# Retention and two feed-forward layers in fp32: state products on four quarters of the array, first-layer weights loaded in 64-row halves, a clamp with two engines to choose from, and a planner with spread deadlines

## The chip, the cores and the metric

The kernel runs on one core of a Trainium2 chip. The metric is device time in microseconds (us): 588.45 us for the kernel before, the median of three runs (588.27 to 588.46). This document names the engines as the profile does: PE multiplies matrices (PEld is its weight load), DVE, ACT and POOL work element by element, SP issues most of the DMAs. PSUM, the memory into which PE writes, has eight banks of 128 rows by 512 fp32 columns.

## The reference

Linear attention with decay (2 sequences, 8 heads, 768 tokens, head size 64), in blocks of 64 tokens, and then two feed-forward layers over 1536 tokens of width 512:

```python
for b in range(nb):
    intra = np.einsum('bhic,bhjc->bhij', qb, kb) * Dmask[None]
    intra = np.einsum('bhij,bhjd->bhid', intra, vb)
    inter = np.einsum('bhid,bhde->bhie', qb * lam_pow[None], kv_state)
    out[:, :, sl] = intra + inter
    kv_state = lam_block[None, :, None, None] * kv_state + np.einsum('bhsd,bhse->bhde', kb_dec, vb)
...
h = x @ w_in                                   # 512 -> 2048
g = np.where(h >= 1, h, np.where(h <= -1, 0.0, (h + 1) ** 2 / 4.0))
x = g @ w_out                                  # 2048 -> 512
...
a = x @ w_a ; b = x @ w_b                      # 512 -> 1536
out = (a * b) @ w_out2                         # 1536 -> 512
```

The weights come as 64-bit floats, and the kernel itself makes 32-bit floats of them.

## The kernel before, in words

**Attention** goes in 12 chunks of 128 tokens, six for each sequence. For a chunk `c`, `att_scores` multiplies keys and queries of the eight heads into two banks, `att_scale` makes the decayed keys `kd` and queries `qd`, `att_mask` multiplies the scores by the decay (`pm`), `att_state` adds the chunk's key-value product to the running state, and `att_out` makes the output: first the product of values and masked scores, then, for all but the first chunk of each sequence (ten of the twelve), the **state products**, eight matmuls of a head's 64x64 state with 64x128 of `qd`. Heads of even and odd number lie on rows 0 to 63 and 64 to 127; the state product of a head uses one 64x64 quarter of the array, and the two quarters on its diagonal are used by turns. All eight heads go into one bank. The output is then split into a high part (`hi`, a cast) and a rest (`lo`, a subtraction), so that the feed-forward layers can multiply fp32 as three products of fp32r parts (`mm3`).

**Feed-forward.** Columns 0 to 511 of the first layer are made by `h_bank` (tiles `ft` 0 to 3, token blocks `nb` 0 to 2; 12 matmuls 128x512 each), for blocks 0 and 1 in between the chunks of the attention. `gate` turns a bank into `g`: a clamp to -1..1, a square, and the larger of that and `h`; `keep_parts` splits the result. `y_bank` multiplies with the second weights. Later columns and the second layer use `seven`, Strassen's seven products, on two token blocks at once, with half-width (256) products for the third block. Weights are loaded by `load_w` (512 KB each, one DMA into a `raw` buffer) and turned to fp32 parts by `weight` (two ACT, three DVE and one POOL operation, and a split).

**What sets the order.** The kernel records every operation as a step with the engines that can do it and a cost, and `Plan.place` then writes out a fixed order for each engine: PE may pick among its next `LOOK` products, the others take what has the earliest deadline (`deadlines`). Buffers are handed out by the planner too: seven PSUM banks (`ps`), pools of 128x512 buffers (`t`, `r`, and `early`, which later becomes `late`), and four `raw` buffers. All `in_att` and weight loads are issued by SP, one after the other. At the start, 40 matmuls of a zero buffer (`warm`, into `words`) stand ready as fillers, of which the planner places those that fit.

Two things matter for reading rows: `tt` records all tensor-tensor steps (L334), `copy` all casts and copies (L338), `mm` all matmuls (L353), so that tiles tell them apart; and an fp32 matmul of the attention shows as two MATMUL records, so the eight of a state product are a row of 16.

Of the kernel before, what the change touches and what calls it, by code (L numbers as in the profile page):

```python
# [12 lines left out]
I32 = mybir.dt.int32  # L13
U32 = mybir.dt.uint32
ACTF = mybir.ActivationFunctionType
# [3 lines left out]
CH = 128  # L19
# [10 lines left out]
HIGH_MAX = struct.unpack("f", struct.pack("I", 0x47EFFFFF))[0]  # L30
HIGH_MIN = struct.unpack("f", struct.pack("I", 0x38000000))[0]

POOLS = {"t": 30, "r": 32, "raw": 4, "ps": 7}
SHARED = 12
LOOK = 6
SPARE, SLOPE = 2, 7.0
AHEAD = 50
NEAR, NEAR_PE = 0.25, 0.4
WIDE = {512: 0.2267, 256: 0.12}
HOP = 0.07  # L40


class Buf:
# [36 lines left out]
class Plan:  # L80
# [35 lines left out]
    def deadlines(self):  # L116
        clock = 0.0
        for s in self.steps:
            if s.ways[0][0] == "PE":
                s.late = clock  # L120
                clock += 0.0 if s.filler else s.ways[0][1]
        users = {}
        for s in self.steps:
            for b in s.bufs:
                if b.kind == "ps":
                    users.setdefault(b, []).append(s)
        bound = {}
        for i, (b, _) in enumerate(self.banks):
            if i + POOLS["ps"] < len(self.banks):
                for s in users[b]:  # L130
                    bound[s] = min(bound.get(s, 1e9), self.banks[i + POOLS["ps"]][1].late)
        for s in reversed(self.steps):
            if s.ways[0][0] != "PE":
                t = min([a.late + a.lead[s] for a in s.after] + [clock + 5, bound.get(s, 1e9)])
                s.late = 0.0 if s.urgent else t - s.ways[0][1] - HOP

    def place(self, free, late, closes, ends, lookahead, reserve):

# [3 lines left out]
        at = {"PE": 0.8, "DVE": 0.8, "ACT": 0.4, "POOL": 0.8, "SP": 0.0}  # L142
        pools = {k: [(0.0, t) for t in ts] for k, ts in free.items()}
        pe = deque(s for s in self.steps if s.ways[0][0] == "PE" and not s.filler)
        lag, port, dma, side = 0.0, {"DVE": 0.0, "POOL": 0.0}, 3.5, 3.5
# [7 lines left out]
        def options(s, window, sparing=True):  # L153
            kinds = {}
            for b in s.bufs:
                if b.slot is None:
                    kinds[b.kind] = kinds.get(b.kind, 0) + 1
            given = 0.0
            for k, n in kinds.items():
                have = sorted(x[0] for x in usable(k))  # L160
                if len(have) < n:
                    return
                given = max(given, have[n - 1])
            soon = {}
            for e, cost, *more in s.ways:
                begin = max([at[e], given] + [x.done if x.engine == e else x.end + HOP - s.lead[x] for x in s.before])
                lock = e in port and more and more[0]
                wait = max(0.0, port["POOL" if e == "DVE" else "DVE"] - begin - 0.1) if lock else 0.0
                slack = s.late + lag - begin
                if s.filler:  # L170
                    yield e, begin, 99, cost, s
                    continue
                if e == "PE":
                    if s not in window or window[s] and kinds.get("ps", 0) > len(pools["ps"]) - (0 if s.early else 2):
                        continue
                    yield e, begin, window[s], cost, s
                    continue
                if sparing and any(k in kinds and len(usable(k)) - kinds[k] < reserve(k, slack) for k in ("t", "r")):
                    continue
                if s.horizon is not None and slack > s.horizon:  # L180
                    begin = s.late + lag - s.horizon
                soon[e] = begin + cost + wait
                if len(soon) > 1:
                    e0, cost0 = s.ways[0][:2]
                    first = soon[e0] + sum(x.ways[0][1] for x in ready if x.ways[0][0] == e0 and x.late < s.late)
                    if first < max(soon[e], s.late + lag + cost0 - 1.0):
                        continue
                yield e, begin, s.late, cost + wait, s

# [17 lines left out]
        while waiting:  # L207
# [27 lines left out]
            if len(way) > 3:  # L235
                if e == "SP":
                    dma = max(dma, begin + 1.4) + way[3] / 388e3
                    s.end = dma + (2.0 if way[3] > 4e5 else 0.5)
# [27 lines left out]
def retention_ffn_kernel(ctx: ExitStack, tc: tile.TileContext, lam, att, w1i, w1o, w2ab, w2o, out):  # L266
# [44 lines left out]
    def bank():  # L311
        return View(Buf("ps"))

    def f_(v):
        return v.of(lambda t: t.bitcast(F32))
# [70 lines left out]
    def small(e, o, ins, emit, cost=0.17, **kw):  # L386
        return plan.step([(e, cost)], o if isinstance(o, list) else [o], ins, lambda _: emit(), **kw)
# [91 lines left out]
    small("DVE", half, [], lambda: nc.vector.memset(half()[:, 0:1], 0.5), 0.1)  # L479
# [75 lines left out]
    def heads(v, h, width):  # L555
        return v.of(lambda t: t[:, h * width:(h + 1) * width])
# [59 lines left out]
        state[c + 1] = st  # L616

    def att_out(c):
        cc = c % CPB
        o = bank()  # L620
        kws = []
        for pr in range(H // 2):
            for e in range(2):
                kws.append(dict(out=o.of(lambda t, e=e, pr=pr: t[64 * e:64 * e + 64, pr * CH:(pr + 1) * CH]),
                                lhsT=heads(ck[c][3], 2 * pr + e, D), rhs=heads(pm[c][e], pr, CH),
                                start=(pr == 0), stop=(cc == 0 and pr == H // 2 - 1)))
        mm(kws, 1.02, [o], [ck[c][3], *pm[c]])
        if cc:
            kws = []
            for pr in range(H // 2):  # L630
                for e in range(2):
                    cut = lambda t, e=e, pr=pr: t[64 * e:64 * e + 64, pr * CH:(pr + 1) * CH]
                    s = state[c].of(lambda t, e=e, pr=pr: t[64 * e:64 * e + 64, pr * D:(pr + 1) * D])
                    kws.append(dict(out=o.of(cut), lhsT=s, rhs=qd[c].of(cut), start=False, stop=(pr == H // 2 - 1)))
            mm(kws, 1.02, [o], [state[c], qd[c], o])
        nb, t0 = c // 4, (c % 4) * CH
        o4 = o.of(lambda t: t.rearrange("p (a i) -> p a i", a=KT))
        hi, lo = (View(blocks[nb], lambda t, i=i: t[:, :, i, t0:t0 + CH], [(k, i, c % 4) for k in range(KT)])
                  for i in range(2))
        copy(hi, o4)  # L640
        tt(lo, o4, f_(hi), ALU.subtract)

    def x_view(nb, k):
        return [View(blocks[nb], lambda t, k=k, i=i: t[:, k, i], [(k, i, q) for q in range(4)]) for i in range(2)]
# [12 lines left out]
    wt, sw = {}, {}  # L657

    def load_w(key):
        raw = View(Buf("raw"))  # L660
        load(raw, srcs[key[0]][key[1]].bitcast(I32), 524288)
        return raw

    def weight(key, raw, horizon):
# [46 lines left out]
    def gate(ps, ft, nb, in_bank=False, half_=None):  # L711
        n = 512 if half_ is None else 256
        r = new() if half_ is None else cols(new(), 0, n)
        fast = ps.buf.kind != "ps"
        plan.step([("DVE", dve(n), fast)], [r], [ps],
                  lambda e: ts_(out=r(), in0=ps(), scalar1=-1.0, scalar2=1.0, op0=ALU.max, op1=ALU.min))  # L716
        plan.step([("ACT", act(n) + 0.1)], [r], [r, half],
                  lambda e: nc.scalar.activation(out=r(), in_=r(), func=ACTF.Square, scale=0.5, bias=half()[:, 0:1]))  # L718
# [10 lines left out]
        split(v, *(halves(x)[half_] for x in gt[key]), n=256)  # L729

    def h_bank(ft, nb):
        gate(product_in("1i", ft, nb), ft, nb, nb < 2)

    ts = {}

# [321 lines left out]
```

## Time and profile before

| | |
|---|---|
| median of the runs | 588.45 us |
| profiled execution, device time | 588.46 us |
| its span, first to last instruction | 586.5 us |
| mean granted clock of PE | 0.996 of full speed |
| PE busy | 577.1 us (98%) |
| POOL, DVE, ACT busy | 478.3, 432.5, 293.9 us |
| read from and written to memory | 47.71 and 3.15 MB |

The profiled execution is as long as the median, and 1.96 us of it lie outside the span. A matmul's record is longer than its turn on the array, since the next one starts before it has ended; so PE's 98% say that it rarely sat with nothing at all, and not that no time can be taken out of it.

### The profile page before, as it was taken

What the parts mean: (1) busy time and instruction counts of PE and PEld (TensorE: products, weight loads), DVE (VectorE), ACT (ScalarE), POOL (GpSimd) and SP (SyncE); (2) the same over time, 40 slices, a digit from 0 to 9 for tenths busy, and PEclk for the clock granted to TensorE, in tenths of its full rate; (3) what the DMA queues carried; (4) which work ended last, traced back from release to release, by engine and by line L of the source; (5) the groups of instructions that cost most, each with busy time, mean ns of one, the idle gap of its engine ahead of it and who ended that gap; (6) DMA issues with size and microseconds to landing.
All of it is one profiled execution on the core that took longest, in us unless ns stands there. A gap on an engine that the chain in (4) does not pass through costs nothing.

```text
span 586.5 us, 9377 instructions
## 1 busy us (share of the span) xinstructions
PE 577.1 (98%) x3403; PEld 487.2 (83%) x3403; DVE 432.5 (74%) x751; ACT 293.9 (50%) x558; POOL 478.3 (82%) x454
## 2 busy tenths in 40 slices
PE   7999999999999999999999999999999999999997
PEld 5788778888788888888888888888888888888885
DVE  7788884059988897888788968785795685685454
ACT  1665665557836663566565475454254164253110
POOL 7899899998778857896999899899699499589640
PEclk8999999999999999999999999999999999999999
DMA  8975241003024102410121232231232131100005
GB/s 289 396 254 189 98 143 37 1 2 122 23 72 145 56 17 73 148 68 0 37 72 37 73 100 80 84 105 63 73 109 71 37 108 39 71 1 0 2 36 180
DMA packets 18911, 51.47 MB, mean 88 GB/s; under 512 B 2224, under 2 KB 3248, under 8 KB 18864
## 3 DMA queue, kind: packets, MB, share of 16 engines
q1 hardware_dynamic: 18144, 50.34, 25.0%
q8 instruction: 27, 0.44, 0.3%
q10 hardware_dynamic: 720, 0.53, 0.3%
q14 instruction: 20, 0.16, 0.1%
HBM read 47.71 MB, written 3.15 MB: 87 GB/s over the span
## 4 chain that ended last, share of the span: by engine, by line
PE 92%; DVE 4%; DMA 2%; ACT 1%; issue 1%; POOL 0%; DVEq 0%; POOLq 0%
PE ps L353 92%; DVE t L334 1%; DMA t<-in_att 1%; DMA lamb<-in_lam 1%; DVE t L716 1%; DVE ps L334 0%; ACT t L718 0%; DVE r L334 0%; POOL powers L424 0%; ACT r L338 0%; DVE block L334 0%; ACT block L338 0%; DVE words L675 0%; DVE words L677 0%; PE words L353 0%
## 5 line engine op out<-in xcount | busy, mean ns | idle before, releaser
L334 DVE TENSOR_TENSOR t<-t,ps 128x512 f32<-128x512 f32 (+1 forms) x324 | 185.1, 585 | 88.2 <-PE ps L353 64.6
L353 PE MATMUL ps<-r,r 128*128 128x512 f32 (+1 forms) x821 | 219.2, 365 | 0.1
L334 POOL TENSOR_TENSOR t<-t,t 128x256 f32<-128x256 f32 (+2 forms) x151 | 155.3, 1044 | 22.7 <-DVE t L680 19.5
L353 PEld LDWEIGHTS ps<-r,r 128*128 128x128 f32 x821 | 144.6, 189 | 25.2 <-ACT r L338 0.4
L353 PE MATMUL ps<-block,r 128*128 128x512 f32 (+1 forms) x652 | 145.3, 351 | 0.7 <-ACT block L338 0.7
L353 PE MATMUL ps<-r,late 128*128 128x512 f32 (+1 forms) x475 | 144.3, 363 | 0.6 <-DVE t L334 0.4
L334 POOL TENSOR_TENSOR r<-t,r 128x512 fp32r<-128x512 f32 (+1 forms) x105 | 119.0, 1146 | 23.8 <-ACT r L338 20.6
L353 PEld LDWEIGHTS ps<-block,r 128*128 128x128 f32 x652 | 110.6, 189 | 18.8 <-ACT block L338 0.9
L338 ACT CAST r<-t 128x512 fp32r<-128x512 f32 (+1 forms) x142 | 76.8, 562 | 68.9 <-DVE t L334 37.1
L353 PEld LDWEIGHTS ps<-r,late 128*128 128x128 f32 x475 | 84.1, 189 | 15.6 <-DVE t L334 1.1
L353 PE MATMUL ps<-block,late 128*128 128x512 f32 (+1 forms) x356 | 81.8, 337 | 0.0
L353 PE MATMUL ps<-late,r 128*128 128x512 f32 x219 | 79.3, 390 | 0.0
L670 ACT ACTIVATE words<-raw 128x512 f32<-128x512 f32 x68 | 43.6, 641 | 59.6 <-DVE t L680 58.9
L334 POOL TENSOR_TENSOR r<-t,late 128x512 fp32r<-128x512 f32 (+1 forms) x51 | 57.6, 1132 | 16.0 <-ACT late L338 12.7
L338 ACT CAST late<-t 128x512 fp32r<-128x512 f32 (+1 forms) x81 | 44.7, 560 | 44.0 <-DVE t L334 25.1
L353 PEld LDWEIGHTS ps<-block,late 128*128 128x128 f32 x356 | 60.2, 189 | 7.8
L675 DVE TENSOR_SCALAR words<-words 128x512 f32<-128x512 f32 x68 | 47.2, 695 | 18.7 <-ACT words L670 17.8
L338 ACT COPY t<-ps 128x512 f32<-128x512 f32 (+2 forms) x62 | 31.7, 515 | 48.6 <-PE ps L353 46.9
L680 DVE SCALAR_TENSOR_TENSOR t<-raw,words 128x512 int32<-128x512 int32 x66 | 45.0, 683 | 13.9 <-POOL t L334 12.5
L353 PE MATMUL ps<-late,late 128*128 128x512 f32 x141 | 52.5, 390 | 0.0
L718 ACT ACTIVATE t<-t,half 128x512 f32<-128x512 f32 (+1 forms) x59 | 36.4, 634 | 27.5 <-DVE t L716 27.0
L353 PEld LDWEIGHTS ps<-late,r 128*128 128x128 f32 x219 | 41.1, 188 | 8.5
(110 smaller groups left out, 538.1 us busy)
## 6 DMA issues: line engine op xcount, KB each, us to landing
raw<-in_w2ab SPq DMA_DIRECT2D x24, 512.0 KB, 3.2
t<-in_att SPq DMA_DIRECT2D x36, 256.0 KB, 5.4
raw<-in_w1i SPq DMA_DIRECT2D x16, 512.0 KB, 3.3
raw<-in_w1o SPq DMA_DIRECT2D x16, 512.0 KB, 3.3
raw<-in_w2o SPq DMA_DIRECT2D x12, 512.0 KB, 3.3
early<-in_att SPq DMA_DIRECT2D x10, 256.0 KB, 6.1
out<-t SPq DMA_DIRECT2D x8, 256.0 KB, 2.0
out<-t SPq DMA_DIRECT2D x4, 128.0 KB, 1.7
```

The source lines that it names most:

```text
L334: plan.step(ways, [o], [x, y], lambda e: engine[e].tensor_tensor(out=o(), in0=x(), in1=y(), op=op))
L338: (nc.scalar.copy if e == "ACT" else nc.vector.tensor_copy)(o(), x())
L353: return lambda e: nc.tensor.matmul(**{k: v() if isinstance(v, View) else v for k, v in kw.items()})
L670: lambda e: nc.scalar.activation(out=words(), in_=f_(high)(), func=ACTF.Abs), horizon)
L675: lambda e: ts_(out=words(), in0=words(), scalar1=HIGH_MIN, scalar2=HIGH_MAX, op0=ALU.max, op1=ALU.min))
L680: lambda e: nc.vector.scalar_tensor_tensor(out=vi(), in0=high(), scalar=-0x40000000, in1=wi(), op0=ALU.bitwise_and, op1=ALU.bitwise_or))
L716: lambda e: ts_(out=r(), in0=ps(), scalar1=-1.0, scalar2=1.0, op0=ALU.max, op1=ALU.min))
L718: lambda e: nc.scalar.activation(out=r(), in_=r(), func=ACTF.Square, scale=0.5, bias=half()[:, 0:1]))
```

## The change

Six edits:

1. `att_out` writes a chunk's output into two banks, one for even and one for odd heads, and places the eight state products on all four 64x64 quarters of the array by turns. Evictions (`hi`, `lo`) become two of 256 columns where they were one of 512.
2. For that, features lie otherwise on rows: a row of `blocks` holds a feature of the first or the second half of the heads. The first layer's weights must follow, so `load_w` loads each `1i` weight with two DMAs of 64 rows and 256 KB.
3. The clamp in `gate` can go to ACT, as two Relu operations of its own, where it went to DVE alone.
4. `h_bank` keeps the result of `gate` in SBUF for all token blocks, not in its bank for blocks 0 and 1.
5. Pools: `t` 32 (30), `r` 30 (32). Constants of the planner: `LOOK` 4 (6), `SPARE` 1 (2), `AHEAD` 40 (50), `NEAR` 0.12 (0.25), and its rules for banks, for the second engine of a step and for DMAs.
6. `deadlines` adds to each deadline a number from a fixed sequence, of another width for each 30 us of the plan (`DRAWS`).

```diff
     def att_out(c):
         cc = c % CPB
-        o = bank()
+        o = [bank(), bank()]
+        places = [(e, hh, p2, lambda t, hh=hh, p2=p2: t[64 * hh:64 * hh + 64, p2 * CH:(p2 + 1) * CH])
+                  for p2 in range(2) for hh in range(2) for e in range(2)]
...
+            for e, hh, p2, cut in places:
+                pr = 2 * hh + p2
+                s, q = (v.of(lambda t, e=e, pr=pr, w=w: t[64 * e:64 * e + 64, pr * w:(pr + 1) * w])
+                        for v, w in ((state[c], D), (qd[c], CH)))
+                kws.append(dict(out=o[e].of(cut), lhsT=s, rhs=q, start=False, stop=(p2 == 1)))
+            mm(kws, 0.55, o, [state[c], qd[c], *o])
...
-        copy(hi, o4)
-        tt(lo, o4, f_(hi), ALU.subtract)
+        for e in range(2):
...
+            copy(hi, o2, 256)
+            tt(lo, o2, f_(hi), ALU.subtract, 256)
...
     def load_w(key):
-        raw = View(Buf("raw"))
-        load(raw, srcs[key[0]][key[1]].bitcast(I32), 524288)
+        raw = View(Buf("raw"), keys=(0, 1))
+        src = srcs[key[0]][key[1]].bitcast(I32)
+        if key[0] == "1i":
+            for hh in range(2):
+                half_ = raw.of(lambda t, hh=hh: t[64 * hh:64 * hh + 64].rearrange("d (e w) -> d e w", e=2), (hh,))
+                load(half_, src.rearrange("(e d) (hh w) -> hh d e w", e=2, hh=2)[hh], 262144)
+        else:
+            load(raw, src, 524288)
...
-        plan.step([("DVE", dve(n), fast)], [r], [ps],
-                  lambda e: ts_(out=r(), in0=ps(), scalar1=-1.0, scalar2=1.0, op0=ALU.max, op1=ALU.min))
+        def clamp(e):
+            if e == "DVE":
+                ts_(out=r(), in0=ps(), scalar1=-1.0, scalar2=1.0, op0=ALU.max, op1=ALU.min)
+                return
+            for i, x in ((1, ps), (2, r)):
+                nc.scalar.activation(out=r(), in_=x(), func=ACTF.Relu, scale=-1.0, bias=half()[:, i:i + 1])
+        clamped = plan.step([("DVE", dve(n), fast), ("ACT", 2 * act(n))], [r], [ps, half], clamp)
...
-        gate(product_in("1i", ft, nb), ft, nb, nb < 2)
+        gate(product_in("1i", ft, nb), ft, nb, False)
...
+        for s in self.steps:
+            if s.ways[0][0] != "PE" and not s.urgent:
+                draw, spread = DRAWS[min(max(int(s.late // STRETCH), 0), len(DRAWS) - 1)]
+                if draw:
+                    s.late += spread * (((s.n + 1) * (2 * draw + 1) * 2654435761 % 2**32 >> 8) % 1000 / 1000 - 0.5)
```

What moves in the written order is shown at three places.

**SP, the loads of the first chunks and weights** (`t` and `early` take `in_att`, `raw` takes weights). Before, from the thirteenth load on:

```order
L349 DMA t_88<-in_att 128x512
L349 DMA raw_127<-in_w1i 128x1024
L349 DMA t_89<-in_att 128x512
L349 DMA t_90<-in_att 128x512
L349 DMA t_91<-in_att 128x512
L349 DMA t_93<-in_att 128x512
L349 DMA raw_128<-in_w1i 128x1024
L349 DMA raw_129<-in_w1i 128x1024
L349 DMA raw_130<-in_w1i 128x1024
L349 DMA early_148<-in_att 128x512
L349 DMA early_149<-in_att 128x512
L349 DMA t_74<-in_att 128x512
```

Now, from the same load on:

```order
L364 DMA raw_127<-in_w1i 64x2x512 x2
L364 DMA t_88<-in_att 128x512
L364 DMA t_89<-in_att 128x512
L364 DMA t_90<-in_att 128x512
L364 DMA t_91<-in_att 128x512
L364 DMA t_92<-in_att 128x512
L364 DMA raw_128<-in_w1i 64x2x512 x2
L364 DMA raw_129<-in_w1i 64x2x512 x2
L364 DMA raw_130<-in_w1i 64x2x512 x2
L364 DMA early_143<-in_att 128x512
L364 DMA early_144<-in_att 128x512
L364 DMA early_146<-in_att 128x512
```

The first weight moved ahead of one `in_att` load, and each weight is two DMAs. Up to the last row shown, SP has issued 20 loads of `in_att` and four weights in both programs.

**PE, up to the first `h_bank` product** (`128x128` are scores, two banks for each chunk; `64x128` are state products; `block_154` is the first token block). Before, the end of chunk 4's scores, chunk 5's, and `h_bank`:

```order
L353 MATMUL ps_134<-t_91,t_93 128x128
L353 MATMUL ps_133<-t_91,t_93 128x128
L353 MATMUL ps_132<-early_149,t_74 128x128
L353 MATMUL ps_136<-early_149,t_74 128x128
L353 MATMUL ps_132<-early_149,t_74 128x128
L353 MATMUL ps_136<-early_149,t_74 128x128
L353 MATMUL ps_132<-early_149,t_74 128x128
L353 MATMUL ps_136<-early_149,t_74 128x128
L353 MATMUL ps_132<-early_149,t_74 128x128
L353 MATMUL ps_136<-early_149,t_74 128x128
L353 MATMUL ps_135<-block_154,r_95 128x512 x4
L353 MATMUL ps_135<-block_154,r_96 128x512 x4
```

Now, the last four state products of chunk 3 and chunk 5's scores; the next row is the first `block_154` product:

```order
L368 MATMUL ps_133<-t_83,t_93 64x128
L368 MATMUL ps_135<-t_83,t_93 64x128
L368 MATMUL ps_133<-t_83,t_93 64x128
L368 MATMUL ps_135<-t_83,t_93 64x128
L368 MATMUL ps_131<-early_146,early_144 128x128
L368 MATMUL ps_136<-early_146,early_144 128x128
L368 MATMUL ps_131<-early_146,early_144 128x128
L368 MATMUL ps_136<-early_146,early_144 128x128
L368 MATMUL ps_131<-early_146,early_144 128x128
L368 MATMUL ps_136<-early_146,early_144 128x128
L368 MATMUL ps_131<-early_146,early_144 128x128
L368 MATMUL ps_136<-early_146,early_144 128x128
```

In both, chunk 5's scores stand ahead of the first `block_154` product, behind the state products of chunks 1 to 3; the loads that they need are the last two rows of SP's list (`early_149` and `t_74` before, `early_144` and `early_146` now). What moved is chunk 4's scores, which now stand ahead of chunk 3's output, and the state products write two banks by turns where one row `x8` wrote one.

**PE, the end of the attention** (`64x128` are the output of chunk 11; `block_156` is the third token block, made of chunks 8 to 11; `r,r` products are `y_bank`). Before:

```order
L353 MATMUL ps_134<-t_67,t_83 64x128 x8
L353 MATMUL ps_135<-block_156,r_95 128x512 x4
L353 MATMUL ps_135<-block_156,r_96 128x512 x4
L353 MATMUL ps_135<-block_156,r_95 128x512 x4
L353 MATMUL ps_136<-r_99,r_113 128x512
L353 MATMUL ps_136<-r_103,r_117 128x512
```

Now, with the 48 `y_bank` matmuls begun that stand ahead of the first `block_156` row:

```order
L368 MATMUL ps_135<-t_77,early_150 64x128
L368 MATMUL ps_137<-r_103,r_114 128x512
L368 MATMUL ps_137<-r_108,r_117 128x512
L368 MATMUL ps_137<-r_107,r_121 128x512
L368 MATMUL ps_137<-r_111,r_123 128x512
```

The product that needs chunk 11's split now comes after four banks of `y_bank`, 48 matmuls, where it came first.

## Rows read from the trace of the kernel before

**Rows 1.** The page's first part: engine, busy us (share of span), instructions.

```profile
span 586.5 us, 9377 instructions
PE 577.1 (98%) x3403; PEld 487.2 (83%) x3403; DVE 432.5 (74%) x751; ACT 293.9 (50%) x558; POOL 478.3 (82%) x454
```

**Rows 2.** The chain that ended last: start us, us, what.

```profile
17.33 7.36 DMA t<-in_att
...
24.74 12.17 PE ps L353 x136
...
36.93 28.91 PE ps L353 x300
...
75.14 0.59 ACT block L338
...
75.78 71.00 PE ps L353 x342
...
320.93 261.94 PE ps L353 x1368
```

**Rows 3.** PE's waits over the span: us in total, times, longest.

```profile
PE ps L353 <- DMA t<-in_att: 2.2, 2, 1.3
PE ps L353 <- ACT block L338: 0.7, 1, 0.7
```

**Rows 4.** Stretches of the start: busy us by engine, PEclk, DMA share, GB/s.

```profile
core 0: us, PE busy (x) PEld busy (x) DVE busy (x) ACT busy (x) POOL busy (x), PEclk, DMA share, GB/s
4.80:8.20 3.40, 2.12 (x34) 1.53 (x33) 1.25 (x7) 0.09 (x1) 3.10 (x2) 1.00 1.02 394
8.20:11.60 3.40, 3.40 (x42) 3.23 (x40) 2.77 (x6) 0.12 (x1) 2.85 (x4) 0.50 1.05 390
11.60:15.50 3.90, 3.43 (x64) 3.05 (x62) 3.81 (x7) 1.46 (x6) 3.82 (x4) 1.00 1.05 395
15.50:21.90 6.40, 6.40 (x124) 5.54 (x120) 5.47 (x10) 5.28 (x12) 4.90 (x5) 1.00 1.04 401
21.90:25.30 3.40, 2.07 (x34) 1.71 (x32) 3.37 (x7) 3.10 (x8) 2.06 (x2) 1.00 1.06 387
```

**Rows 5.** PE's timeline around 24 us: start us, us, what, [idle before <-releaser].

```profile
19.73 3.67 PE L353 MATMUL ps<-t,t 128*64 128x64 f32 x64
24.74 1.16 PE L353 MATMUL ps<-early,t 64*128 64x128 f32 x16 [1.33 <-DMA t<-in_att]
25.83 0.50 PE L353 MATMUL ps<-block,r 128*128 128x512 f32 x1
```

**Rows 6.** PE's timeline, chunk 11's output and the product after it.

```profile
73.15 0.27 PE L353 MATMUL ps<-early,t 128*64 128x128 f32 x1
73.25 0.27 PE L353 MATMUL ps<-t,t 128*64 128x128 f32 x1
73.26 0.27 PE L353 MATMUL ps<-early,t 128*64 128x128 f32 x1
73.36 0.27 PE L353 MATMUL ps<-t,t 128*64 128x128 f32 x1
...
74.01 1.09 PE L353 MATMUL ps<-t,t 64*64 64x128 f32 x16
75.78 0.50 PE L353 MATMUL ps<-block,r 128*128 128x512 f32 x1 [0.69 <-ACT block L338]
```

**Rows 7.** Stretches after the start, columns as in rows 4.

```profile
25.60:75.80 50.20, 49.39 (x551) 39.52 (x547) 41.43 (x70) 30.77 (x66) 45.85 (x38) 1.00 0.57 198
75.80:147.00 71.20, 71.20 (x346) 60.16 (x347) 38.48 (x63) 41.19 (x77) 66.57 (x64) 1.00 0.17 57
147.00:210.00 63.00, 62.87 (x316) 52.88 (x315) 55.13 (x97) 38.13 (x71) 52.32 (x49) 1.00 0.21 70
210.00:272.00 62.00, 61.95 (x311) 52.61 (x311) 52.39 (x92) 35.89 (x67) 46.47 (x44) 1.00 0.21 68
272.00:314.00 42.00, 41.95 (x194) 34.87 (x193) 35.84 (x62) 26.62 (x53) 37.46 (x35) 1.00 0.15 51
314.00:321.00 7.00, 6.54 (x43) 5.70 (x41) 6.89 (x12) 3.56 (x9) 6.41 (x8) 1.00 0.01 2
```

**Rows 8.** Groups by form: x, busy us, mean ns of one.

```profile
L334 DVE TENSOR_TENSOR t<-t,ps 128x256 f32<-128x256 f32 x122 | 50.2, 418 | 8.2 <-PE ps L353 4.5 <-ACT words L670 0.8 <-issue 0.4
L334 DVE TENSOR_TENSOR block<-ps,block 128x512 fp32r<-128x512 f32 x16 | 10.8, 683 | 0.7 <-ACT block L338 0.7
```

**Rows 9.** POOL's timeline in the attention.

```profile
23.24 1.04 POOL L573 TENSOR_TENSOR t<-early,kdf 128x512 f32<-128x512 f32 x1 [1.58 <-DMA early<-in_att]
24.24 1.28 POOL L334 TENSOR_TENSOR r<-t,r 128x512 fp32r<-128x512 f32 x1
25.47 1.30 POOL L334 TENSOR_TENSOR early<-early,early 128x512 f32<-128x512 f32 x1
```

More of the change, by code (lines that the diff above doesn't have):

```diff
@@ L31 @@
 HIGH_MIN = struct.unpack("f", struct.pack("I", 0x38000000))[0]
-POOLS = {"t": 30, "r": 32, "raw": 4, "ps": 7}
+POOLS = {"t": 32, "r": 30, "raw": 4, "ps": 7}
 SHARED = 12
[L35 to L38, printed above, removed]
+LOOK = 4
+SPARE, SLOPE = 1, 7.0
+AHEAD = 40
+NEAR, NEAR_PE = 0.12, 0.4
+FEW, LEAN = 1, 4.0
 WIDE = {512: 0.2267, 256: 0.12}
 HOP = 0.07
+STRETCH = 30
+DRAWS = [
+    (262, 0.5), (880, 2), (847, 8), (427, 8), (643, 2), (204, 2), (444, 8), (719, 4), (593, 8), (0, 0.5),
+    (213, 1), (0, 8), (849, 8), (0, 4), (986, 2), (0, 1), (683, 0.5), (0, 2), (657, 4),
+]
 class Buf:
@@ L144, in place @@
         pe = deque(s for s in self.steps if s.ways[0][0] == "PE" and not s.filler)
-        lag, port, dma, side = 0.0, {"DVE": 0.0, "POOL": 0.0}, 3.5, 3.5
+        lag, port, dma, side, fetch = 0.0, {"DVE": 0.0, "POOL": 0.0}, 4.05, 4.6, 1.35
         waiting = {s: len(s.before) for s in self.steps}
@@ L173, in options @@
                 if e == "PE":
-                    if s not in window or window[s] and kinds.get("ps", 0) > len(pools["ps"]) - (0 if s.early else 2):
+                    if s not in window or window[s] and kinds.get("ps", 0) > len(pools["ps"]) - (FEW if s.early else 2):
                         continue
@@ L185, in options @@
                     first = soon[e0] + sum(x.ways[0][1] for x in ready if x.ways[0][0] == e0 and x.late < s.late)
-                    if first < max(soon[e], s.late + lag + cost0 - 1.0):
+                    if first < max(soon[e], s.late + lag + cost0 - LEAN):
                         continue
@@ L237, in place @@
                     dma = max(dma, begin + 1.4) + way[3] / 388e3
-                    s.end = dma + (2.0 if way[3] > 4e5 else 0.5)
+                    if dma > 13.2:
+                        dma, fetch = dma + fetch, 0.0
+                    s.end = dma + 0.5
                 else:
@@ L478, in retention_ffn_kernel, with constants @@
     small("DVE", full, [], lambda: nc.vector.memset(full(), 1.0))
-    small("DVE", half, [], lambda: nc.vector.memset(half()[:, 0:1], 0.5), 0.1)
+    def constants():
+        for i, x in enumerate((0.5, 1.0, 2.0)):
+            nc.vector.memset(half()[:, i:i + 1], x)
+    small("DVE", half, [], constants, 0.3)
     by_head = lambda t: t.rearrange("p (h n) -> p h n", h=H)
@@ L619, in att_out @@
         cc = c % CPB
-        o = bank()
+        o = [bank(), bank()]
+        places = [(e, hh, p2, lambda t, hh=hh, p2=p2: t[64 * hh:64 * hh + 64, p2 * CH:(p2 + 1) * CH])
+                  for p2 in range(2) for hh in range(2) for e in range(2)]
         kws = []
[L622 to L626, printed above, removed]
@@ L627, in att_out @@
-        mm(kws, 1.02, [o], [ck[c][3], *pm[c]])
+        for e, hh, p2, cut in sorted(places, key=lambda x: (x[2], x[0], x[1])):
+            pr = 2 * hh + p2
+            kws.append(dict(out=o[e].of(cut), lhsT=heads(ck[c][3], 2 * pr + e, D), rhs=heads(pm[c][e], pr, CH),
+                            start=(p2 == 0), stop=(cc == 0 and p2 == 1)))
+        mm(kws, 1.02, o, [ck[c][3], *pm[c]])
         if cc:
             kws = []
[L630 to L635, printed above, removed]
@@ L636, in att_out @@
-        nb, t0 = c // 4, (c % 4) * CH
-        o4 = o.of(lambda t: t.rearrange("p (a i) -> p a i", a=KT))
-        hi, lo = (View(blocks[nb], lambda t, i=i: t[:, :, i, t0:t0 + CH], [(k, i, c % 4) for k in range(KT)])
-                  for i in range(2))
-        copy(hi, o4)
-        tt(lo, o4, f_(hi), ALU.subtract)
+            for e, hh, p2, cut in places:
+                pr = 2 * hh + p2
+                s, q = (v.of(lambda t, e=e, pr=pr, w=w: t[64 * e:64 * e + 64, pr * w:(pr + 1) * w])
+                        for v, w in ((state[c], D), (qd[c], CH)))
+                kws.append(dict(out=o[e].of(cut), lhsT=s, rhs=q, start=False, stop=(p2 == 1)))
@@ L643, in x_view @@
+            mm(kws, 0.55, o, [state[c], qd[c], *o])
+        nb, t0 = c // 4, (c % 4) * CH
+        for e in range(2):
+            o2 = o[e].of(lambda t: t[:, 0:256].rearrange("p (a i) -> p a i", a=2))
+            hi, lo = (View(blocks[nb], lambda t, i=i, e=e: t[:, 2 * e:2 * e + 2, i, t0:t0 + CH],
+                           [(2 * e + p2, i, c % 4) for p2 in range(2)]) for i in range(2))
+            copy(hi, o2, 256)
+            tt(lo, o2, f_(hi), ALU.subtract, 256)
     def x_view(nb, k):
@@ L714, in gate @@
         fast = ps.buf.kind != "ps"
-        plan.step([("DVE", dve(n), fast)], [r], [ps],
-                  lambda e: ts_(out=r(), in0=ps(), scalar1=-1.0, scalar2=1.0, op0=ALU.max, op1=ALU.min))
+        def clamp(e):
[5 more added lines that the diff above has]
+        clamped = plan.step([("DVE", dve(n), fast), ("ACT", 2 * act(n))], [r], [ps, half], clamp)
         plan.step([("ACT", act(n) + 0.1)], [r], [r, half],
-                  lambda e: nc.scalar.activation(out=r(), in_=r(), func=ACTF.Square, scale=0.5, bias=half()[:, 0:1]))
+                  lambda e: nc.scalar.activation(out=r(), in_=r(), func=ACTF.Square, scale=0.5,
+                                                 bias=half()[:, 0:1] if clamped.engine == "DVE" else 0.0))
         v = ps if in_bank else r
```

## The prediction

> **What bounds the kernel now.** I read the page's first part first: PE is busy for 577.1 of 586.5 us, the next engine, POOL, for 478.3 [rows 1]. The chain that ended last says the same by place. From 75.78 us on it is PE but for a few short pieces, in runs of up to 262 us, and from 24.74 us to 65.8 too; only ahead of 24.69 us does something else carry it, a load of `in_att` that took 7.36 us from issue to landing [rows 2]. So every us of PE work that goes after 25 us is a us of time, while what goes ahead of it is worth nothing unless that load lands sooner. The waits agree: PE waited 2.2 us for `in_att`, 1.33 of it at 24.74 us, and 0.7 once for a cast into `block` [rows 3, 5, 6]. The stretches after that show little more to win by a better order: in 147 to 321 us PE is without any matmul for 0.13, 0.05, 0.05 and 0.46 us [rows 7], 0.69 together. (Records overlap, so a wait shorter than a record's rest is not seen.)
>
> Then the load. From 4.8 to 25.3 us the DMA engines are full, at 387 to 401 GB/s in each stretch [rows 4]. The load that PE waits for is the last of 20 loads of 256 KB and four weights of 512 KB: 28 pieces of 262,144 bytes, 7.34 MB, in the queue order of both programs. At 395 GB/s a piece takes 0.66 us, and 28 take 18.6. PE's wait at 24.74 us is thus a matter of bytes and rate, and not of when SP issues.
>
> **The change, part by part.**
>
> State products on four quarters. The trace has pairs on two quarters at a time, and in such a pair the two records start 0.01 us apart and the next pair 0.11 later (73.15 and 73.25/73.26, then 73.36) [rows 6]; that is the product of values and masked scores, and the state products fit it: 16 records in 1.09 us, less 0.27 for the last one's length, is 0.82 for seven steps, 0.117 each, the first of them longer. On four quarters the eight matmuls, two records each, are four steps where they were eight: 4 x 0.11 = 0.44 us less for a chunk. No row shows four quarters at work, so the bounds are 0 (the second pair waits for the first) and 0.44. I take 0.44, since the two quarters of a pair already run side by side at no loss that a row shows. Ten chunks have them. Those of chunks 1 to 3 stand ahead of chunk 5's scores, which wait for the load; PE would be done 1.3 us sooner, at 22.1 where it was at 23.4 [rows 5], and wait until 24.74 all the same. Seven are left: **-3.05 us**.
>
> The end of the attention. Before, the product of `block_156` at 75.78 us came right behind chunk 11's output and waited for its cast: the output's last matmuls ended at 75.10 (74.01 and 1.09), and PE had nothing for 0.69 us [rows 6]. Now 48 matmuls of `y_bank` stand in between. They need weights and gates, not chunk 11. POOL makes the last of these parts, and may be late: between the first decayed keys at 23.24 us and the low part of the fourth weight it had 41 steps before, and has 36 now, seven of them the shorter L573. At 1.00 and 1.23 us from start to start [rows 9] that is 48.8 us before and 42.7 now, 6 less, where PE comes 3.05 sooner. So the cover holds, and the sum takes **-0.7 us**; without it nothing is won here.
>
> Halves of 64 rows. Same bytes, same place ahead of chunk 5's loads, but no row has a transfer of fewer than 128 rows. Below: by bytes, 0.66 us for each half, no change. Above: if 64 rows take what 128 rows of the same length would carry, 1.32 us, 0.66 more for each of eight halves: 5.3 us more wait. I take no change: loads of 2 KB a row and of 4 KB a row (the weights) run at one rate, 390 to 401 GB/s with either in flight [rows 4], so bytes are what counts in the rows there are. The later twelve weights lie where the DMAs are busy for 0.16 to 0.57 of the time [rows 7] and can be late by more than that. SP issues 16 DMAs more; it is the bytes that it waits for.
>
> The clock. PE ran at 0.50 of full speed from 8.2 to 11.6 us, behind a stretch in which it was busy 2.12 of 3.4 us; behind 21.9 to 25.3, with 2.07 busy, it kept 1.00 [rows 4]. [...] Below: no fall, 0. Above: one stretch of 3.4 us at half speed, 1.7 us. Two stretches so alike went both ways, so I take the middle: **+0.85 us**.
>
> Evictions in two pieces. A 512-wide subtraction is 683 ns, two of 256 are 2 x 418 [rows 8]: 0.15 us more DVE for a chunk, 1.8 in all, and about as much on ACT. DVE is idle for 8.8 and ACT for 19.4 of the 50.2 us of that stretch [rows 7], which hides it; uncovered, each would hold a bank and PE would wait up to 0.15 us for a chunk, 1.2 in the eight that come after 25 us. Clamps on ACT, `gate` results in SBUF, and three constants in place of one on DVE go with this: DVE and ACT have the room, and PE reads none of it within microseconds.
>
> Pools, constants, deadlines. The number and size of PE's products stay, and behind the attention their order does but for two places where a full and a half-width product swap. What can change is who is late. Below: the 0.69 us of idle PE go away; above: as many new ones as the rivals say. I take 0.
>
> Start and tail: nothing of the work ahead of 24.7 us is on the path but the load; the last products, sums and stores are the same.
>
> **Sum**, from the profiled execution's own 588.46 us (span 586.5, 1.96 around it), which is the median: 588.45 - 3.05 - 0.7 + 0.85 = 585.55, so **585.5 us**.
>
> **Rivals.**
>
> (a) Half-row loads are slow. Then the wait at 24.74 us grows by up to 5.3 us, and with so long a wait the clock surely falls: 588.45 - 3.75 + 1.7 + 5.3 = 591.7. It makes the kernel slower by over 0.2% (1.2 us) once the halves are 3.2 us late together, that is from 1.06 us a half. For it: nothing in the trace limits a load by its rows, but all of them fill all 128, and the start has no slack for it at all. Against: one rate for two row lengths. [...]
>
> (b) Four quarters don't overlap more than two did. The 3.05 us and the shorter wait are gone, with the clock as it was: 588.45 - 0.7 = 587.75. Against it: pairs at 0.01 us [rows 6].
>
> (c) New waits in the attention. A chunk takes six banks with its `h_bank` where it took five of the seven, and PE comes sooner while POOL had only 4.4 us idle of 50.2 [rows 7]. If one in three of the eight chunks and gates after 25 us costs PE an eviction of 0.7 us, 2 us go: 587.5; the gain is gone at 3.
>
> **Chances.** 0.55 for the forecast (0.53 of it faster by over 0.2%, which is about what a measurement can tell here and means under 587.27), 0.25 for (a) (0.20 slower, above 589.63; 0.05 within, where halves cost a little), 0.08 for (b) (within), 0.12 for (c) (0.04 faster, 0.05 within, 0.03 slower). So faster 0.57, same 0.20, slower 0.23. The range begins at 583.0: no fall of the clock (584.7), the idle 0.69 gone, and part of the first three chunks' 1.3 us won after all. It goes up to 590.5, past the estimate for (a) and short of its worst; 0.2 lie outside. The forecast's own range is 583.0 to 586.5.
>
> **What the profile would show.** State products: 16 records in 0.6 to 0.65 us where it was 1.09; if that is 1.09, (b). The first `block_154` product at 25.8 us; if it starts at 28 or later, behind a longer wait for `in_att`, (a), and the issue of the weights' halves shows it. PEclk of 0.50 in the stretch behind that wait, or not. The first `y_bank` product with no wait ahead of it, near 72 us (75.78 less 0.7 and 3.05) plus what the clock cost. PE idle between 26 and 72 us of more than 1 us in total: (c). The prediction is wrong if chunk 5's scores start later than 26 us, or if the state products are no shorter.

## The result and the profile after

The changed kernel is slower: 593.91 us (median of 4 runs, 593.21 to 594.09) against 588.46 for the kernel before beside it (588.27 to 588.5), a ratio of 1.0091 with a 95% interval of 1.0074 to 1.0109. The profiled execution took 593.81 us, with a span of 591.9, 5.4 more than in [rows 1]. The forecast was 585.5 with a range up to 590.5: wrong in sign, and outside the range. One of ten executions of the diagonal kernel below took 1474.91 us and is left out of its ratio.

The page's first part, and its row of PE's clock and of GB/s in 40 slices of 14.8 us:

```profile
span 591.9 us, 9487 instructions
...
PE 575.2 (97%) x3408; PEld 483.2 (82%) x3408; DVE 459.3 (78%) x780; ACT 296.2 (50%) x571; POOL 476.4 (80%) x445
...
PEclk9989999999999999999999999999999999999999
...
GB/s 258 282 296 236 135 89 61 37 36 72 37 71 131 78 8 48 166 72 0 37 37 72 72 91 93 103 110 104 35 108 73 35 77 101 1 2 0 2 36 178
```

PE is busy for 1.9 us less than in [rows 1] and idle for 16.7 us where it was 9.4: the loss is idle time. The chain of work that ended last (start us, us, what) says where, beside [rows 2]:

```profile
13.35 9.89 DMA raw<-in_w1i
23.25 7.55 DMA early<-in_att
30.94 119.57 PE ps L368 x902
```

A half of a `w1i` weight was on its way for 9.89 us, the `in_att` load behind it came late with it, and PE's long run starts at 30.94 us where it was 24.74. PE's timeline there (start us, us, what, idle before), which answers to [rows 5]:

```profile
22.18 2.78 PE L368 MATMUL ps<-t,t 64*128 64x128 f32 x48 [1.79 <-DVE t L349]
30.94 2.08 PE L368 MATMUL ps<-early,early 64*128 64x128 f32 x16 [5.98 <-DMA early<-in_att]
32.95 3.60 PE L368 MATMUL ps<-block,r 128*128 128x512 f32 x12
```

Chunk 5's scores wait 5.98 us instead of 1.33, and take 2.08 us instead of 1.16; the first `block_154` product starts 7.12 us later. The stretches of the start (busy us by engine, PEclk, DMA share, GB/s), beside [rows 4]:

```profile
8.20:11.60 3.40, 3.40 (x66) 2.85 (x66) 2.34 (x5) 0.53 (x2) 1.65 (x3) 1.00 1.05 390
11.60:15.50 3.90, 2.37 (x43) 1.78 (x40) 3.87 (x8) 1.44 (x5) 3.76 (x4) 1.00 1.08 257
15.50:21.90 6.40, 4.89 (x106) 3.94 (x102) 6.05 (x14) 3.43 (x10) 4.52 (x5) 1.00 1.06 291
21.90:25.30 3.40, 2.78 (x48) 2.28 (x48) 0.58 (x2) 0.82 (x2) 1.85 (x2) 1.00 1.07 225
...
27.50:34.20 6.70, 3.26 (x19) 2.88 (x20) 4.53 (x6) 3.59 (x10) 5.56 (x5) 0.50 0.96 327
```

Once the halves are in flight, the DMA engines count as full (shares above 1) and move 225 to 291 GB/s where they moved 387 to 401. The stretch from 15.5 to 21.9 us holds two rates; cut where the rate changes, the same time reads:

```profile
12.05:15.40 3.35, 1.82 (x28) 1.36 (x28) 3.32 (x7) 1.44 (x5) 3.21 (x4) 1.00 1.07 232
15.40:18.10 2.70, 2.70 (x60) 2.23 (x58) 2.60 (x6) 1.80 (x4) 1.70 (x2) 1.00 1.05 385
18.10:26.90 8.80, 5.07 (x104) 4.08 (x99) 5.35 (x12) 2.84 (x9) 4.77 (x4) 1.00 1.07 229
```

The rate is low around the first weight's halves and around the other six, and full between them. At 225 GB/s, the rate from 21.9 to 25.3 us, a half of 262,144 bytes takes 1.17 us, against 0.66 for the same bytes into 128 rows. And behind the long wait PE ran at 0.50 of its full clock from 27.5 to 34.2 us.

What the change was to save came. A state product and what follows the last one, beside [rows 6]:

```profile
78.93 0.67 PE L368 MATMUL ps<-t,early 64*64 64x128 f32 x16
79.52 1.66 PE L368 MATMUL ps<-r,r 128*128 128x512 f32 x6
```

It is 0.67 us where it was 1.09, and `y_bank` follows with no wait. The idle 0.46 us at 314 us [rows 7] is gone too (the stretch 5.3 us later):

```profile
319.30:326.30 7.00, 7.00 (x51) 6.62 (x50) 6.05 (x13) 3.92 (x8) 6.50 (x8) 1.00 0.23 75
```

But two stalls are new, far from every line of the diff that I had priced. The timelines of PE, DVE and POOL at the first; the second, at 503.5 us, is alike:

```profile
454.81 0.40 PE L368 MATMUL ps<-r,late 128*128 128x256 f32 x2
456.33 1.65 PE L368 MATMUL ps<-block,r 128*128 128x512 f32 x6 [1.12 <-DVE t L349]
...
451.46 4.22 DVE L353 CAST late<-t 128x512 fp32r<-128x512 f32 x1
455.60 1.60 DVE L349 TENSOR_TENSOR t<-t,ps 128x512 f32<-128x512 f32 x3
...
450.92 1.28 POOL L349 TENSOR_TENSOR t<-t,t 128x512 int32<-128x512 int32 x1
452.17 1.29 POOL L349 TENSOR_TENSOR r<-t,late 128x512 fp32r<-128x512 f32 x1
453.41 1.29 POOL L349 TENSOR_TENSOR r<-t,r 128x512 fp32r<-128x512 f32 x1
454.66 0.73 POOL L349 TENSOR_TENSOR t<-t 128x256 f32<-128x256 f32 x1
455.83 1.28 POOL L349 TENSOR_TENSOR r<-t,late 128x512 fp32r<-128x512 f32 x1 [0.43 <-DVE late L353]
```

A cast from SBUF to SBUF on DVE lasts from 451.46 until 455.68, 0.3 us after POOL's run of four instructions ends; the eviction behind it on DVE, for which PE waits, comes as late. The changed plan has six such casts on DVE, and the kernel before had none.

### The profile page after: what moved, and what is told of

The parts are those of the page before. It is cut to its first block, busy times and chain, and to the rows that moved or that the text cites. A ratio compares the mean times of both kernels' runs of the same rounds, so it can differ in the third digit from the quotient of the medians.

```text
span 591.9 us, 9487 instructions
## 1 busy us (share of the span) xinstructions
PE 575.2 (97%) x3408; PEld 483.2 (82%) x3408; DVE 459.3 (78%) x780; ACT 296.2 (50%) x571; POOL 476.4 (80%) x445
## 4 chain that ended last, share of the span: by engine, by line
PE 86%; DMA 5%; DVE 3%; POOL 2%; issue 2%; ACT 1%; SPq 0%; DVEq 0%; POOLq 0%
PE ps L368 86%; DMA t<-in_att 2%; DMA raw<-in_w1i 2%; DMA early<-in_att 1%; POOL r L349 1%; DVE t L349 1%; POOL t L349 1%; POOL late L349 1%; DVE words L708 0%; DVE t L711 0%; DVE words L706 0%; DVE t L749 0%; ACT words L701 0%; ACT late L353 0%; SPq L364 0%
## 5 line engine op out<-in xcount | busy, mean ns | idle before, releaser
L349 DVE TENSOR_TENSOR t<-t,ps 128x256 f32<-128x256 f32 (+1 forms) x329 | 186.4, 585 | 75.3 <-PE ps L368 65.7
L368 PE MATMUL ps<-r,r 128*128 128x512 f32 (+1 forms) x863 | 237.6, 366 | 0.1
L349 POOL TENSOR_TENSOR t<-t,t 128x512 int32<-128x512 int32 (+2 forms) x152 | 159.7, 1066 | 26.6 <-DVE t L711 12.7
L368 PE MATMUL ps<-r,late 128*128 128x512 f32 (+1 forms) x383 | 111.3, 357 | 0.0
L368 PE MATMUL ps<-late,r 128*128 128x512 f32 x269 | 96.3, 390 | 0.1
L368 PEld LDWEIGHTS ps<-r,late 128*128 128x128 f32 x383 | 66.8, 189 | 10.9 <-POOL late L349 0.2
L368 PEld LDWEIGHTS ps<-late,r 128*128 128x128 f32 x269 | 50.5, 188 | 10.7 <-ACT late L353 0.5
L349 POOL TENSOR_TENSOR late<-t,r 128x512 fp32r<-128x512 f32 (+1 forms) x37 | 48.5, 1317 | 10.4 <-ACT r L353 10.4
L703 ACT ACTIVATE t<-raw 128x512 int32<-128x512 uint32 x67 | 43.7, 667 | 13.2 <-DMA raw<-in_w2ab 5.6
L349 POOL TENSOR_TENSOR r<-t,late 128x512 fp32r<-128x512 f32 (+1 forms) x37 | 44.0, 1196 | 5.7 <-ACT late L353 5.2
```

The source lines that it names most:

```text
L349: plan.step(ways, [o], [x, y], lambda e: engine[e].tensor_tensor(out=o(), in0=x(), in1=y(), op=op))
L703: lambda e: nc.scalar.activation(out=c(), in_=low.of(lambda t: t.bitcast(U32))(), func=ACTF.Copy, scale=2.0**-29), horizon)
```

## The experiments

Theory: the halves cost the start because of the rows that they go to; the state products save what was forecast; the two casts cost the rest. Rivals: the cut source, the number of loads, or the new order of the work for the first; two banks instead of four quarters for the second; another lateness of DVE for the third. Each kernel ran beside the kernel before, which took 588.34 to 588.42 us (median) there.

| Kernel | us, median | ratio to before, 95% interval |
|---|---|---|
| changed, one load for each `w1i` weight | 585.99 | 0.9964 [0.9951, 0.9977] |
| changed, halves with a source of 4 KB a row | 593.22 | 1.0082 [1.0069, 1.0095] |
| changed, two loads of 128 rows | 586.53 | 0.9978 [0.9966, 0.9991] |
| one load, state products in another order | 586.08 | 0.9953 [0.9938, 0.9967] |
| one load, casts on ACT | 583.78 | 0.9925 [0.9912, 0.9939] |
| before, with halves alone | 595.01 | 1.0117 [1.0103, 1.013] |
| one load, state products on the diagonal | 588.99 | 1.0011 [1.0002, 1.0021] |
| changed, loads into every second row | 586.03 | 0.9971 [0.996, 0.9981] |
| one load, casts on ACT, chunk 5's loads sooner | 582.57 | 0.99 [0.9884, 0.9917] |

**One load for each weight.** The `w1i` tiles are laid out beforehand in the order of rows and columns in which the halves would have put them, so that one load of 128 rows does.

```diff
-                half_ = raw.of(lambda t, hh=hh: t[64 * hh:64 * hh + 64].rearrange("d (e w) -> d e w", e=2), (hh,))
-                load(half_, src.rearrange("(e d) (hh w) -> hh d e w", e=2, hh=2)[hh], 262144)
+                half_ = raw.of(lambda t: t, (hh,))
+                plan.step([("SP", 0.4, False, 262144)], [half_], [],
+                          lambda e, hh=hh: nc.sync.dma_start(out=raw(), in_=src) if hh == 0 else None)
...
-        "w1i": tiles(inputs["moe_w_in"]),
+        "w1i": tiles(inputs["moe_w_in"]).reshape(-1, 2, D, 2, 256).transpose(0, 3, 2, 1, 4).reshape(-1, 128, 512),
```

> The changed kernel with each w1i weight loaded by one 512-KB transfer into all 128 rows (its rows laid out in the new order in memory beforehand), every other instruction on every engine in the same order. Theory 1, a transfer into 64 rows takes about 1.2 us for 256 KB: chunk 5's scores start near 24.7 us, the first block_154 product at 25.8 instead of 32.95 (7.1 us), the first product runs at full clock (0.75): 593.8 - 7.1 - 0.75 = 586.0 us; with the clock's fall of my forecast up to 587.7. Theory 2, something else in the new order or the number of loads makes the start late, not the rows: within 0.5 us of 593.8.

585.99 us, 7.92 less than the changed kernel. One of its stretches:

```profile
11.60:15.50 3.90, 2.38 (x38) 1.72 (x32) 3.87 (x9) 2.59 (x7) 3.76 (x5) 1.00 1.05 394
```

and PE's timeline:

```profile
24.55 1.16 PE L368 MATMUL ps<-early,early 64*128 64x128 f32 x16 [1.53 <-DMA early<-in_att]
25.64 3.02 PE L368 MATMUL ps<-block,r 128*128 128x512 f32 x12
```

Theory 1 holds; all that the halves cost is back. The clock kept its upper level in this execution (1.00 from 21.9 to 31 us); over the seven runs the mean granted clock was 0.999 or 1.0 in four (584.42 to 585.99 us) and 0.996 or 0.997 in three (586.34 to 587.86). Only the profiled execution shows where a clock fell, so that it fell behind this wait in those three is likely and not shown; a kernel below with the same start shows it there (0.50 from 26.3 to 29.6 us).

**What in the halves costs.** Three kernels change the halves' shape alone (each with the rows laid out beforehand): 64 rows from 4 KB in one piece, 128 rows of half the columns, and every second row.

```diff
...
+                half_ = raw.of(lambda t, hh=hh: t[64 * hh:64 * hh + 64], (hh,))
+                load(half_, src[64 * hh:64 * hh + 64], 262144)
...
```

> The changed kernel, each w1i weight still in two transfers into 64 rows, but each row from 4 KB that lie together in memory (no second stride of 2 KB). Theory 1, the 64 rows are what costs: halves still 1.2 us apart, 593.8 us. Theory 2, the cut source (two pieces of 2 KB a row) costs: halves 0.66 us apart, start as in the kernel before, 586.0 us.

```diff
...
+                half_ = raw.of(lambda t, hh=hh: t[:, 512 * hh:512 * hh + 512], (hh,))
+                load(half_, src[:, 512 * hh:512 * hh + 512], 262144)
...
```

> The changed kernel, each w1i weight in two transfers of 256 KB, each into all 128 rows and half of the columns. Theory 1, the 64 rows are what costs: 0.66 us each, first block_154 product near 25.8, 586.0 us. Theory 2, twice the number of loads of half the size costs: 593.8 us.

```diff
...
+                half_ = raw.of(lambda t, hh=hh: t.rearrange("(p h) w -> h p w", h=2)[hh], (hh,))
+                load(half_, src.rearrange("(p h) w -> h p w", h=2)[hh], 262144)
...
```

> The changed kernel, each w1i weight in two transfers of 256 KB into 64 rows, but into every second row from 0 to 126 and then every second from 1 to 127. Theory A, the number of rows costs: halves 1.2 us apart, 593.4 us as with rows 0 to 63. Theory B, it is which rows: a transfer whose rows lie over all 128 takes 0.66 us, 586.0 us. [...]

593.22, 586.53 and 586.03 us. The stretch from 11.6 to 15.5 us, in which the second half of the first weight and the loads behind it fly, for the lower and upper 64 rows:

```profile
11.60:15.50 3.90, 2.64 (x48) 2.02 (x44) 3.87 (x9) 1.44 (x5) 3.76 (x4) 1.00 1.05 261
```

for 128 rows of half the columns:

```profile
11.60:15.50 3.90, 2.64 (x44) 1.88 (x43) 3.87 (x9) 2.69 (x7) 3.76 (x5) 1.00 1.06 388
```

and for every second row:

```profile
11.60:15.50 3.90, 2.37 (x42) 1.78 (x40) 3.87 (x8) 2.47 (x7) 3.76 (x4) 1.00 1.04 393
```

The last column is 261, 388 and 393 GB/s. The last two kernels load 128 and 64 rows at a time and both move about what one load for each weight did (394). So it isn't the number of loads, and it isn't the number of rows either: it is that all 64 are the lower or the upper ones. The cut source costs little: chunk 5's scores start at 30.43 us without it, at 30.94 with it. Theory B holds; the 225 GB/s of the changed kernel are 57% of the 393 here. What in the hardware makes it so is not shown, and no run loads 64 rows in one piece across the middle (32 to 95), so rows on one side of row 64 are not told apart here from rows that merely lie together.

**The halves alone.** The kernel before, with each `w1i` weight's load issued as two.

```diff
-        load(raw, srcs[key[0]][key[1]].bitcast(I32), 524288)
...
+        def both(e):
+            for i in range(2):
+                part = slice(64 * i, 64 * i + 64)
+                engine[e].dma_start(out=raw()[part], in_=src[part])
...
+            plan.step([("SP", 0.4, False, 524288)], [raw], [], both)
...
```

> The kernel before with nothing changed but the w1i weights' loads, each issued as two transfers of 256 KB into rows 0 to 63 and 64 to 127, from 4 KB in one piece for each row. Theory, the halves alone make the start late, by what the changed kernel lost there (7.1 us to the first block_154 product and 0.75 in it): 588.4 + 7.9 = 596.3 us. Rival, they cost only together with the new order of the work: 588.4 us.

595.01 us, 6.67 more than before. PE's timeline:

```profile
29.48 2.08 PE L353 MATMUL ps<-early,t 64*128 64x128 f32 x16 [5.93 <-DMA t<-in_att]
31.48 3.60 PE L353 MATMUL ps<-block,r 128*128 128x512 f32 x12
```

The theory holds and the rival falls: the new order of the work isn't needed for the loss. It is 1.2 us smaller than I wrote, since the scores start at 29.48 and not at 30.94; 0.5 us of that difference is the cut source, and the rest I can't place.

**Whether four quarters are what saves.** First the order alone was changed, so that the two quarters of one half of the output rows come first.

```diff
-            for e, hh, p2, cut in places:
+            for e, hh, p2, cut in sorted(places, key=lambda x: x[1]):
...
```

> The kernel with one load for each w1i weight, and the state products in the order in which only two quarters of the array follow each other (first all of one half of the output rows, then all of the other). Theory, the 0.42 us that each of seven state products is shorter is time of the whole: each takes 1.09 us again and the kernel 7 x 0.42 = 2.95 us more than with one load alone, near 589.0 us. Rival, that time only goes into later waits for evictions: within 0.7 us of the kernel with one load, 586 to 586.7.

586.08 us, and a state product is as short as without it:

```profile
72.79 0.68 PE L368 MATMUL ps<-t,early 64*64 64x128 f32 x16
```

So this undid nothing: the experiment missed its aim and says only that PE does as well with this order (0.68 us, where it was 0.67). In it the first four of the 16 records start within 0.03 us (72.79 to 72.82 us) and the fifth 0.13 us later. The records of one quarter start 0.11 us apart, so I infer that these four are on four quarters, two of them ahead of products that stand earlier in the order; which quarter a record is on, and how it came to start there, no row shows. Then the outputs were put back on the rows where the kernel before had them, with two banks as in the changed kernel; only the diagonal quarters are used.

```diff
-        places = [(e, hh, p2, lambda t, hh=hh, p2=p2: t[64 * hh:64 * hh + 64, p2 * CH:(p2 + 1) * CH])
+        places = [(e, hh, p2, lambda t, e=e, p2=p2: t[64 * e:64 * e + 64, p2 * CH:(p2 + 1) * CH])
...
-                kws.append(dict(out=o[e].of(cut), lhsT=s, rhs=q, start=False, stop=(p2 == 1)))
+                kws.append(dict(out=o[hh].of(cut), lhsT=s, rhs=q, start=False, stop=(p2 == 1)))
...
```

The product of values and masked scores, left out of this cut, moves with them.

> The kernel with one load for each w1i weight, two banks kept, but the output of even and odd heads put back on the lower and upper 64 rows, so that the state products reach only the two quarters on the array's diagonal (and the weights keep their rows as the kernel before had them). Theory, four quarters are what made them short: 1.09 us each, 7 x 0.42 = 2.95 us more, 586.0 + 2.95 = 588.9 us. Rival, two banks are what made them short, or what is saved goes into other waits: 0.67 us each or 586.0 us.

588.99 us, 3.00 more than with four quarters (7 x 0.42 = 2.94). A state product is long again:

```profile
73.64 1.09 PE L368 MATMUL ps<-t,early 64*64 64x128 f32 x16
```

It is the quarters, not the banks, and their time is the whole's time. The product of values and masked scores has no part in it: in chunk 10, from its start to the `h_bank` product behind the state product, PE takes 2.00 us here (67.21 to 69.21) and 1.57 with four quarters (65.01 to 66.58), which is the state product's 0.42.

**The casts on DVE.** The six casts from SBUF to SBUF are issued on ACT, at the same place of the order.

```diff
-            (nc.scalar.copy if e == "ACT" else nc.vector.tensor_copy)(o(), x())
+            inside = x.buf.kind != "ps" and o.buf.kind != "ps"
+            (nc.scalar.copy if e == "ACT" or inside else nc.vector.tensor_copy)(o(), x())
...
```

> The kernel with one load for each w1i weight, and its six casts from SBUF to SBUF that the planner gave to DVE issued on ACT in place of DVE, everything else in the same order. Theory, the two casts that took 4.2 us beside back-to-back POOL work make PE wait twice, 2.3 us together: 586.0 - 2.3 = 583.7 us, no wait of PE of 1.1 us near 447 and 494 us. Rival, DVE was late there for another reason, or ACT is late in its place: within 0.5 us of the kernel with one load.

583.78 us, 2.21 less. PE runs on where it waited 1.1 us, and the cast takes 0.62 us on ACT:

```profile
448.63 0.40 PE L369 MATMUL ps<-r,late 128*128 128x256 f32 x2
448.87 2.26 PE L369 MATMUL ps<-block,r 128*128 128x512 f32 x12
...
443.35 0.62 ACT L354 CAST late<-t 128x512 fp32r<-128x512 f32 x1
```

The theory holds. In the profiled execution, of 585.09 us, the clock fell (0.50 from 26.3 to 29.6 us); another run, of 585.01 us, had the same mean clock, 0.996, and the other three, of 583.29 to 583.78 us, had 0.998 or 0.999.

A cast on DVE is not held so long every time. In the profiled executions of two kernels above (two loads of 128 rows, and the other order), one of the two casts got in behind the first of POOL's four instructions, took 1.00 and 1.05 us, and PE did not wait for it. DVE and POOL in the latter:

```profile
492.59 1.05 DVE L353 CAST r<-t 128x512 fp32r<-128x512 f32 x1
...
493.30 1.50 POOL L349 TENSOR_TENSOR r<-t,r 128x512 fp32r<-128x512 f32 x1
```

Over the seven profiled kernels with these casts, twelve of fourteen were held for 4.2 us. What decides it is not shown. In those two executions the clock had fallen too (a mean of 0.997 in both), so the time of a run doesn't tell by itself what either costs.

**Chunk 5's loads sooner.** SP issues the fourth `w1i` weight three loads later.

```diff
...
+    moved = next(x for x in sp if x[3] is w_step["1i", 3])
+    last = max(placed.index(x) for x in sp if x[3] in (parts_of[5, 0], parts_of[5, 1]))
+    at_ = placed.index(moved)
...
+    placed = placed[:at_] + placed[at_ + 1:last + 1] + [moved] + placed[last + 1:]
...
```

> The kernel with one load for each w1i weight and the six casts on ACT; in addition SP issues the fourth w1i weight behind the last in_att load that chunk 5's scores need, three places later, nothing else moved. Theory, the wait of 1.8 us for in_att at 24.6 us is bytes ahead in the queue: 512 KB less ahead of it bring it 1.3 us sooner, PE waits 0.5 us, and with so short a wait the clock keeps its upper level there in every run (it fell in two of the five runs of the kernel without this, 1.7 us each): 583.4 - 1.3 = 582.1 us, and no run near 585. Rival, the fourth weight, now 2 us later, holds ACT and so the evictions queued behind its first step: what is won at 24.6 us is lost by 40 us, 583.4 or more.

582.57 us in the median, 582.44 to 582.64 over four runs, each at a granted clock of 0.999 or 1.0. PE's and ACT's timelines:

```profile
23.62 1.16 PE L369 MATMUL ps<-early,early 64*128 64x128 f32 x16 [0.48 <-DMA early<-in_att]
24.71 3.02 PE L369 MATMUL ps<-block,r 128*128 128x512 f32 x12
...
24.83 0.67 ACT L712 ACTIVATE early<-raw 128x512 int32<-128x512 uint32 x1 [0.82 <-DMA raw<-in_w1i]
```

The wait is 0.48 us, as forecast, and the scores start 1.02 us sooner than with the weight in front (24.64). ACT does wait for the weight, 0.82 us, and the rival's loss doesn't follow: the start's gain is kept. It is the best version here, 1.0% under the kernel before.

## Why the prediction was wrong

- **Halves of 64 rows, "I take no change: loads of 2 KB a row and of 4 KB a row (the weights) run at one rate, 390 to 401 GB/s with either in flight, so bytes are what counts in the rows there are".** This is the step that failed. Both row lengths in [rows 4] fill all 128 rows, so they say nothing of a load that fills half; their agreement was taken as evidence against rival (a), and it wasn't. Rival (a) is what happened, at about its price for a half: 1.17 us where its bounds were 0.66 and 1.32. Its total, 591.7 at most, was too small. The upper end of the range, 590.5, was set past an estimate for (a) that no run shows; the runs showed 1.17 us a half and 593.91 us in all. The halves by themselves are 8 x 0.51 = 4.1 us, and the scores came 6.20 us late. The rate was 229 to 232 GB/s for 12.15 us, in which 2.8 MB moved, 0.7 more than the eight halves, so loads of `in_att` beside them were slow too; at 395 GB/s these bytes would have taken 5.1 us less, and the rest of the 6.20 I can't place. Against the kernel with one load the scores start 6.39 us later (30.94 and 24.55); with 0.92 and 0.58 us for the clock, below, that is 7.89 of the 7.92 us that one load gives back.
- **State products, -3.05.** Right: 0.42 each instead of 0.44 (seven times 0.44 is 3.08), and 3.00 us in all by the diagonal kernel. The two orders tried in PE's queue made no difference (586.08 and 585.99 us).
- **End of the attention, -0.7.** Right in the trace: no wait ahead of the first `y_bank` product.
- **Clock, +0.85, between 0 and 1.7.** For the start that I forecast (one load) both ends came: the mean clock says that it fell in three of seven runs and kept its level in four, and the median run is one of the four. Behind the wait that really came it stayed low from 27.5 to 34.2 us, and cost 0.92 us in the scores and 0.58 in the product behind them (12 records in 3.60 us, where they take 3.02 at full clock).
- **Evictions in two pieces and clamps, 0.** No run tested these by themselves. The trace puts 1.79 us ahead of 22.18 us down to an eviction, but the late loads are behind that as well: with one load and the same order PE is busy for 6.36 of the 6.40 us from 15.5 to 21.9, where it was 4.89. The two waits of 1.1 us on evictions come from the casts.
- **Pools, constants, deadlines, 0.** The terms that I named were there: the idle 0.69 us after 147 us went away for the most part (0.22 us left between 152.3 and 326.3). What I missed was a change of engine. I looked at the order of PE's products and not at which engine the planner now gives a cast, and put no price on the six casts that moved to DVE. Two of them cost 2.21 us together.

The sum from the experiments, against 588.38: the new plan with two banks +0.61 (588.99, of which the casts are 2.21, so everything else in it is -1.6: the end of the attention 0.69, the late idle time 0.47, and 0.4 that I can't place), four quarters -3.00, halves +7.92: 593.91. It comes out to the last digit because each term is a difference of these medians. With the halves at nothing the forecast of 585.5 would have met 585.99, but by luck in part: the casts' 2.21 us and the 0.9 us that the new plan gave back beyond the end of the attention were both left out, and the clock entered as half of what it costs when it falls.

## What to carry to other kernels

Rows that agree with each other speak only for the range that they cover: look for what all of them share (here, 128 rows) before using them against a rival. A load that must go to 64 rows can take every second of the 128, as here (393 GB/s from 11.6 to 15.5 us, where the halves had 257), or be laid out in memory so that one load fills every row (394). And when a planner's costs change, list which instructions change their engine, not just their place: one copy on DVE beside a run of POOL's work took 4.22 us and held up an eviction, and so PE, by 1.12 us.

## What the runs showed of the hardware

- With transfers of 256 KB into rows 0 to 63 and 64 to 127 in flight the DMA engines moved 257 GB/s from 11.6 to 15.5 us (261 with 4 KB a row in one piece) and 225 from 21.9 to 25.3; with the same bytes into every second row they moved 393 from 11.6 to 15.5 us, and 394 with one load of 128 rows.
- A cast from SBUF to SBUF of 128x512 on DVE took 4.2 us in twelve of fourteen cases when it met POOL in a run of four tensor-tensor instructions on SBUF, and PE then waited 1.1 us; in the changed kernel the two casts (4.22 and 4.24 us) ended 0.3 us after that run did. In the other two cases it took 1.00 and 1.05 us. Of the other four casts of the changed kernel three took 0.42 to 0.43 us; on ACT one took 0.62. So the cast came to its end behind one of POOL's instructions in the two cases, and behind four in a row in the twelve; what in the hardware holds it is not shown.
- State products on 64x64 quarters took 0.68 us for 16 records in an order by halves, 0.67 in turn, and 1.09 when only two quarters are used.
